# Attention scores on 32-row tiles of the array, Q masked by head parity, units of 256 queries, output clamps dropped

## The chip, the cores and the metric

The kernel runs on one core of one Trainium2 chip. The metric is the time of one execution on the device in microseconds (us), given as the median of several executions. Engine names are those of the profile: PE is the matmul engine, PEld its weight load, DVE VectorE, ACT ScalarE, POOL GpSimd. "Granted clock" is the PE clock in the clock records of the profile, with 1.00 for full speed. P·V is the matmul of the attention weights with V.

## The reference, cut to what matters

Two layers, each an attention block and a feed-forward block on the same weights. Inputs are bf16.

```python
def _A_ref(x, wqkv, wo):                  # B=1, S=2048, D=512
    H = 32; Dh = D // H; W = 256          # 32 heads of 16
    q, k, v = ...                         # from x @ wqkv
    scores = einsum("bhqd,bhkd->bhqk", q, k) * (Dh ** -0.5)
    mask = (0 <= idx_q - idx_k) & (idx_q - idx_k < W)   # causal, window of 256
    p = softmax(where(mask, scores, -1e9))
    return einsum("bhqk,bhkd->bhqd", p, v) @ wo         # heads side by side
def _B_ref(x, w1, w2):                    # Dff = 1792
    return relu(x @ w1) @ w2

x = x + _A_ref(layernorm(x), wqkv, wo);  x = x + _B_ref(layernorm(x), w1, w2)   # twice
```

A head has only 16 dimensions, so the contraction of a score matmul is 16 rows long on an array of 128 rows. All of the change turns on that.

## The kernel before

Heads lie 8 to a group `t` of 128 partitions. To score one head at a time with a matmul over all 128 rows, the kernel keeps copies of Q, `Qi`, that are zero in the rows of all other heads. Eight DMAs for each half of a chunk of 512 queries write the 16 live rows of each head into them. A unit of work is one block of 128 queries. Scores go to PSUM, the memory that PE writes its results to (a buffer of 512 fp32 columns there is called a bank below), ACT takes the exponential of eight heads at once, POOL clears what the mask forbids, and PE multiplies with V, which carries a column of ones for the row sums.

```python
    ptp = ...(name="ptp", bufs=5)
    ps_s = ...(name="ps_s", bufs=2, PSUM);   ps_acc = ...(bufs=1, PSUM)
    ps_w = ...(name="ps_w", bufs=1, PSUM)    # warm-up, output projection
    ps_d = ...(name="ps_d", bufs=2, PSUM)    # dense matmuls
    CLS = {"setup": 0, "s": 1, "a": 2, "q": 3, "f": 4}   # priorities: scores before attention before qkv before FFN
    # ... (cut)
    def isolate_q(QT, hfq):
        for j in range(8):
            nc.sync.dma_start(out=Qi[hfq][16 * j:16 * j + 16, :, j, :],
                              in_=QT[16 * j:16 * j + 16, :, hfq * 256:(hfq + 1) * 256])

    def attention_qblock(layer, qb, jq, chk):          # 128 queries
        # ... (cut) for a in range(2): for t in (2a, 2a+1): for kbi in range(3):
                        Sps = ps_s.tile([P, 2, 4, P], FP32, name="Sps")
                        for xh in range(2):
                            nc.tensor.matmul(Sps[:, xh]..., lhsT=KT[:, t, kcols],
                                             rhs=Qih[:, t, 4 * xh:4 * xh + 4, qcols], start=True, stop=True)
                        nc.scalar.activation(pt[:, kbi]..., Sps[:]..., ACT.Exp)
                # ... (cut) two affine_select on POOL, P·V matmuls, reciprocal, multiply into O
            ok1 = ...; ok2 = ...; ok = ...             # DVE: is the row sum within bounds
            nc.gpsimd.tensor_scalar(out=O[:], in0=O[:], scalar1=1.0e18, scalar2=-1.0e18, op0=ALU.min, op1=ALU.max)
            nc.gpsimd.tensor_tensor(out=O3, in0=O3, in1=ok[:]..., op=ALU.mult)

    def attn_post(qb, O):
        nc.sync.dma_start_transpose(out=OT[:], in_=O[:]...)
        ps = ps_w.tile([P, 512], FP32, name="ps_w")    # output projection, its own bank
        # ... (cut) 4 matmuls with wo, add to x
```

While chunk k is in attention, the q, k, v matmuls of chunk k+1 and the FFN of chunk k-1 fill the gaps of PE.

## Time and profile before

| | before |
|---|---|
| median of 2 runs | 642.85 us (641.36 to 644.34) |
| span of the profiled run | 643.3 us |
| mean granted clock | 0.970 |
| six attention stretches | 158.9, 51.5, 39.9, 51.5, 52.2, 52.2 us |
| five dense stretches between them | 31.7, 24.7, 28.5, 24.7, 25.7 us |
| from the last score to the end | 75.5 us |

The stretches are read from the timeline of PE. Where the score matmuls stop for tens of microseconds a dense stretch begins, and where they come back it ends.

These are lines of the page of the kernel before: busy time of each engine in us, then three of its rows of 40 equal slices, in tenths (9 is 90% or more).

```profile
PE 576.2 (90%) x5053; PEld 282.8 (44%) x5053; DVE 321.1 (50%) x701; ACT 368.2 (57%) x407; POOL 367.7 (57%) x391
...
ACT  5667686999850399705870399705894079920000
...
PEclk8968996999999999999999999999999999999998
```

ACT shows the two kinds of stretch: near 9 in attention, near 0 in dense work. After the first quarter the granted clock is full, but for 3.41 us at 578 us and the last 4 us.

The groups of instructions of the kernel before follow. The columns are line, engine, operation, tiles, shape and count, then busy us and mean ns of one, then the idle time ahead of them in us and what ended most of it.

```profile
L225 ACT ACTIVATE pt<-Sps 128x1024 bf16<-128x1024 f32 x360 | 344.8, 1025 | 95.3 <-PE Sps L223 82.8
L223 PE MATMUL Sps<-Qi,KT 128*128 128x512 bf16 x720 | 218.9, 386 | 4.1 <-ACT pt L225 2.8
```

The 386 ns is one matmul from start to end. In the records matmuls overlap, so the cost is the distance from start to start, and the timeline of PE in the kernel before shows it (columns: start, us, engine, line, operation, tiles, count):

```profile
302.64 0.59 PE L223 MATMUL Sps<-Qi,KT 128*128 128x512 bf16 x2
303.07 0.59 PE L346 MATMUL ps_d<-xn2T,w 128*128 128x512 bf16 x2
303.50 0.59 PE L223 MATMUL Sps<-Qi,KT 128*128 128x512 bf16 x2
```

Each pair of 512-column matmuls takes 0.43 us, that is 0.215 us each. A score group and a dense pair cost the same.

The windows of an attention stretch, a dense stretch and the tail of the kernel before follow. The columns are window and length, busy us (count) of PE, PEld, DVE, ACT and POOL, granted clock, share of DMA and GB/s.

```profile
217.00:268.50 51.50, 48.45 (x511) 25.05 (x510) 21.49 (x45) 44.64 (x47) 39.68 (x40) 1.00 0.16 33
268.50:293.20 24.70, 23.24 (x154) 10.60 (x151) 17.31 (x42) 2.29 (x6) 7.17 (x9) 1.00 0.08 19
567.80:643.30 75.50, 64.63 (x333) 28.71 (x329) 32.88 (x61) 1.64 (x4) 13.29 (x20) 0.95 0.21 33
```

An attention stretch has 48.45 us of PE and 44.64 us of ACT in 51.5 us, at full clock. Both are nearly full, so by an estimate from these numbers shortening the scores on PE can gain about 7 us of the 51.5 (51.5 − 44.64) and no more: then ACT is the limit.

### The profile page before, as it was taken

Reading aid. Unit: us, or ns where it says so; the run is one execution under the profiler, and the core shown is the slowest. Engines: PE = TensorE matmul, PEld = TensorE weight load, DVE = VectorE, ACT = ScalarE, POOL = GpSimd, SP = SyncE. Lnnn points to the kernel's source line nnn. Section 1 sums busy time; section 2 is a strip of 40 time slices with the busy share of each in tenths; the row PEclk is TensorE's granted clock in tenths of the full one; section 3 lists DMA queues with packets and bytes.
Section 4 is the critical chain, followed back from the end, with each engine's and each line's share of the span. In section 5 each row is a group of like instructions: output and inputs, shape, how many; then the busy total and the mean of one; then the engine's idle time right before and its main releaser. Section 6 shows DMA issues by size and latency. Waiting matters only on the chain.

```text
span 643.3 us, 12352 instructions
## 1 busy us (share of the span) xinstructions
PE 576.2 (90%) x5053; PEld 282.8 (44%) x5053; DVE 321.1 (50%) x701; ACT 368.2 (57%) x407; POOL 367.7 (57%) x391
## 2 busy tenths in 40 slices
PE   6957979999989999999899999999998899979994
PEld 2323434544544444534453444534454344534442
DVE  2794533544465634476455634475443544436361
ACT  5667686999850399705870399705894079920000
POOL 2168778888861287815872287814887147851200
PEclk8968996999999999999999999999999999999998
DMA  9601121111002110102101110202102210131302
GB/s 316 202 22 34 31 55 42 26 34 43 10 9 42 45 31 10 43 8 50 34 11 41 42 34 11 42 10 52 23 10 57 36 25 9 19 59 16 58 8 39
DMA packets 69217, 27.10 MB, mean 42 GB/s; under 512 B 52512, under 2 KB 68640, under 8 KB 69152
## 3 DMA queue, kind: packets, MB, share of 16 engines
q1 hardware_dynamic: 63984, 19.94, 13.6%
q0 software_dynamic: 2304, 2.10, 2.2%
q10 hardware_dynamic: 2864, 4.19, 1.8%
q8 instruction: 41, 0.67, 0.5%
q14 instruction: 24, 0.20, 0.1%
HBM read 7.86 MB, written 2.10 MB: 15 GB/s over the span
## 4 chain that ended last, share of the span: by engine, by line
PE 32%; POOL 19%; DMA 11%; issue 10%; ACT 8%; DVE 4%; SPq 0%; POOLq 0%; ACTq 0%
DMA OT<-O 9%; ACT pt L225 8%; PE ps_d L353 7%; POOL pt L228 7%; PE Sps L223 5%; PE ps_d L346 5%; POOL O L259 4%; POOL pt L232 4%; PE ps_w L333 3%; PE ps_d L176 3%; PE acc L240 3%; PE ps_d L184 3%; PE ps_d L191 3%; POOL O L257 2%; DMA xn2T<-xnB 1%
## 5 line engine op out<-in xcount | busy, mean ns | idle before, releaser
L225 ACT ACTIVATE pt<-Sps 128x1024 bf16<-128x1024 f32 x360 | 344.8, 1025 | 95.3 <-PE Sps L223 82.8
L223 PE MATMUL Sps<-Qi,KT 128*128 128x512 bf16 x720 | 218.9, 386 | 4.1 <-ACT pt L225 2.8
L228 POOL TENSOR_SCALAR_AFFINE_SELECT pt<-pt 128x1024 bf16<-128x1024 bf16 x128 | 140.3, 1099 | 67.4 <-ACT pt L225 67.1
L232 POOL TENSOR_SCALAR_AFFINE_SELECT pt<-pt 128x1024 bf16<-128x1024 bf16 x112 | 122.2, 1091 | 34.4 <-ACT pt L225 31.4
L240 PEld LDWEIGHTS <-pt 128*128 128x128 bf16 x2880 | 100.2, 96 | 87.6 <-POOL pt L228 38.4
L240 PE MATMUL acc<-Vaug,pt 128*128 128x17 bf16 x2880 | 108.9, 171 | 26.4 <-POOL pt L228 20.7
L346 PE MATMUL ps_d<-xn2T,w 128*128 128x512 bf16 x448 | 123.9, 378 | 0.9 <-DVE hT L348 0.9
L348 DVE TENSOR_SCALAR hT<-ps_d 128x512 bf16<-128x512 f32 x112 | 77.1, 689 | 61.4 <-PE ps_d L346 61.0
L353 PE MATMUL ps_d<-w,hT 128*128 128x512 bf16 x448 | 105.7, 381 | 0.0
L223 PEld LDWEIGHTS <-KT 128*128 128x128 bf16 x720 | 64.3, 97 | 68.5 <-issue 16.8
L334 DVE TENSOR_TENSOR x_sb<-ps_w,x_sb 128x512 f32<-128x512 f32 x32 | 22.1, 692 | 102.2 <-PE ps_w L333 80.8
L353 PEld LDWEIGHTS <-hT 128*128 128x128 bf16 x448 | 43.2, 98 | 50.4 <-issue 1.9
L346 PEld LDWEIGHTS <-w 128*128 128x128 bf16 x448 | 39.8, 97 | 43.2 <-issue 5.7
L333 PE MATMUL ps_w<-wo,OT 128*128 128x512 bf16 x128 | 38.3, 390 | 18.4 <-DMA OT<-O 18.3
L162 POOL TENSOR_SCALAR xnB<-x_sb,rstdB,nbB 128x512 bf16<-128x512 f32 x32 | 24.4, 766 | 42.4 <-DMA xn2T<-xnB 25.5
L247 DVE RECIPROCAL chk<-acc 128x16 f32<-128x16 f32 x64 | 16.4, 256 | 56.8 <-PE acc L240 56.7
L162 POOL TENSOR_SCALAR xnA<-x_sb,rstdA,nbA 128x512 bf16<-128x512 f32 x28 | 21.4, 769 | 40.2 <-DVE nbA L150 37.7
L178 DVE CAST QT<-ps_d 128x512 bf16<-128x512 f32 x32 | 22.0, 689 | 37.2 <-PE ps_d L176 37.2
L147 ACT ACTIVATE lnvB<-mv4B,ln_bias 128x4 f32<-128x4 f32 x8 | 2.4, 296 | 66.2 <-DVE mv4B L143 66.2
L357 POOL DMA_DIRECT2D out_dram<-x_sb x16 | 9.1, 570 | 52.8 <-DVE x_sb L355 37.2
L176 PE MATMUL ps_d<-xnT,wqkv 128*128 128x512 bf16 x128 | 36.4, 399 | 2.6 <-DVE QT L178 1.8
L355 DVE TENSOR_TENSOR x_sb<-ps_d,x_sb 128x512 f32<-128x512 f32 x32 | 22.0, 689 | 28.4 <-PE ps_d L353 25.8
(62 smaller groups left out, 391.5 us busy)
## 6 DMA issues: line engine op xcount, KB each, us to landing
Qi<-QT SPq DMA_DIRECT2D x128, 32.0 KB, 2.0
w<-in_B_w_dram ACTq DMA_DIRECT2D x2, 1792.0 KB, 13.9
xst<-in_A_x_dram SPq DMA_DIRECT2D x4, 512.0 KB, 14.4
out_dram<-x_sb POOLq DMA_DIRECT2D x16, 128.0 KB, 2.3
wqkv<-in_A_wqkv_dram SPq DMA_DIRECT2D x3, 512.0 KB, 13.1
wo<-in_A_wo_dram ACTq DMA_DIRECT2D x1, 512.0 KB, 5.5
OT<-O SPq DMA_TRANSPOSE x32, 2.3
xn2T<-xnB SPq DMA_TRANSPOSE x32, 2.4
```

The source lines that it names most:

```text
L162: nc.gpsimd.tensor_scalar(out=xn[:], in0=x_sb[:, b, :], scalar1=rstd[:, j:j + 1], scalar2=nb[:, j:j + 1], op0=ALU.mult, op1=ALU.add)
L176: nc.tensor.matmul(ps[:], lhsT=wqkv[:, kc, t * P:(t + 1) * P], rhs=xnT[:, kc, :], start=(kc == 0), stop=(kc == KC - 1))
L223: nc.tensor.matmul(Sps[:, xh].rearrange("p j q -> p (j q)"), lhsT=KT[:, t, kcols], rhs=Qih[:, t, 4 * xh:4 * xh + 4, qcols], start=True, st ...
L225: nc.scalar.activation(pt[:, kbi].rearrange("p j q -> p (j q)"), Sps[:].rearrange("p x j q -> p (x j q)"), ACT.Exp)
L228: nc.gpsimd.affine_select(out=pt[:, 2], in_=pt[:, 2], pattern=[[0, 8], [1, P]], compare_op=ALU.is_ge, fill=0.0, base=0, channel_multiplier=-1)
L232: nc.gpsimd.affine_select(out=pt[:, 0], in_=pt[:, 0], pattern=[[0, 8], [-1, P]], compare_op=ALU.is_gt, fill=0.0, base=0, channel_multiplier=1)
L240: mm = nc.tensor.matmul(acc[:, h % 16, :], lhsT=pt[:, kbi, j, :], rhs=Vaug[:, slot(layer, kb), h, :], start=(ii == 0), stop=(ii == len(kbi ...
L259: nc.gpsimd.tensor_tensor(out=O3, in0=O3, in1=ok[:].to_broadcast([P, 32, 16]), op=ALU.mult)
L333: nc.tensor.matmul(ps[:], lhsT=OT[:, kc, :], rhs=wo[:, kc, :], start=(kc == 0), stop=(kc == KC - 1))
L346: nc.tensor.matmul(ps[:, n0:n1], lhsT=w1[:, kc, f * P:(f + 1) * P], rhs=xnT[:, kc, n0:n1], start=(kc == 0), stop=(kc == KC - 1))
L348: nc.vector.tensor_relu(hT[:, f, n0:n1], ps[:, n0:n1])
L353: nc.tensor.matmul(ps[:], lhsT=hT[:, f, j * P:(j + 1) * P], rhs=w2[:, f, :], start=(f == 0), stop=(f == NF - 1))
```

## The change

The intent is to stop computing with rows that are zero. A score matmul is to use 32 rows of the array alone, and two of them on different rows are to run side by side. A row tile of 32 holds two heads, so Q is written twice, once with the odd heads zeroed and once with the even ones, both by DVE with a parity mask; the `Qi` copies, their clearing and their DMAs go. The unit grows to 256 queries of 8 heads. The checks and clamps of the output go; the flag at the end, which sends a bad input through a slow exact path, stays. `acc` gets a second PSUM buffer in the place of `ps_w`: the output projection now rotates through `ps_d`.

```diff
-    ptp = ... bufs=5        ps_acc = ... bufs=1       ps_w = ... bufs=1
+    ptp = ... bufs=3        ps_acc = ... bufs=2
 # ... (cut)
-        Qi = [const.tile([P, 4, 8, 256], BF16, name=f"Qi{i}") for i in range(2)]
+        nc.gpsimd.iota(pidx[:], pattern=[[0, 1]], base=0, channel_multiplier=1)
+        # ... (cut) par[:, 0], par[:, 1]: 1 or 0 by bit 16 of the partition number
 # ... (cut)
-            nc.vector.tensor_copy(QT[:, t, :], ps[:])
+            for e in range(2):
+                nc.vector.tensor_scalar(out=Qz[:, t, e, :], in0=ps[:], scalar1=par[:, e:e + 1], scalar2=None, op0=ALU.mult)
-    def isolate_q(QT, hfq): ...
-    def attention_qblock(layer, qb, jq, chk):
+    def attention_pair(layer, m, jm, Qz, chk):
+        for t in range(4):
+                for x in kinds:
+                    for rp in range(2):
+                        Sps = ps_s.tile([P, 2, 512], FP32, name="Sps")
+                        # ... (cut) parts: one of 256 queries, or two of 128
+                        for kb, col, qo, w in parts:
+                            for r in range(2):
+                                rows = slice(32 * (2 * rp + r), 32 * (2 * rp + r) + 32)
+                                nc.tensor.matmul(Sps[:, r, col:col + 2 * w], lhsT=KT[rows, t, kslice(kb)],
+                                                 rhs=Qz[rows, t, :, q0 + qo:q0 + qo + w], start=True, stop=True)
+                        nc.scalar.activation(pt[:, x, 2 * rp:2 * rp + 2, lo:512], Sps[:, :, lo:512], ACT.Exp)
+            # ... (cut) four affine_select, P·V into acc [P, 2, 8, 17]
-            ok1 = ...  ok2 = ...  ok = ...
-            nc.gpsimd.tensor_scalar(out=O[:], ... op0=ALU.min, op1=ALU.max)
-            nc.gpsimd.tensor_tensor(out=O3, in0=O3, in1=ok[:]..., op=ALU.mult)
 # ... (cut) attn_post
-        ps = ps_w.tile([P, 512], FP32, name="ps_w")
+        ps = ps_d.tile([P, 512], FP32, name="ps_d")
```

## The prediction

> **What bounds the kernel now.** The page shows PE busy 90% of 643.3 us, ACT and POOL 57%, but this averages two kinds of stretch. Gaps between score matmuls in the timeline give six attention stretches (158.9, 51.5, 39.9, 51.5, 52.2, 52.2 us) separated by five dense stretches (24.7 to 31.7 us, no scores, ACT idle), and a 75 us tail. Start to start, a 512-column matmul takes 0.215 us and a P·V matmul 0.026 us. A 48-exp stretch holds 46 us of PE stream (48 × 2 × 0.215 scores, 25.4 other), and 48 exps at 0.945 us each (8 in 7.55 us) are 45.4 us of ACT. Both are equally loaded; the stretch takes 52. The first (132 exps) has PE 121, ACT 125, and takes 159. PE streams sum to 539 us; about 104 is waiting.
>
> **What the change does.**
> - Scores: 720 matmuls of 512 columns become 480 of 512 and 480 of 256, the same columns, two side by side on different 32-row groups. [...] No trace here has row tiles. The compiled order has about 350 separate score groups among 128-row work, so nearly every group pays two switches. I estimate 0.40 us per group (0.3 to 0.5)[...]. That saves 10 us, not 75.
> - ACT is unchanged, so attention stretches cannot go below 45.4 us (125 in the first).
> - POOL loses two output operations (0.62 + 1.05 us, 32 times, 53 us), which delay the output transpose and the selects.
> - DVE writes Q twice (+0.69 us, 32 times) and drops three check operations (36 us in all).
> - The Qi clearing (7.1 us ACT) and 128 Qi DMAs go: first exp about 4 us earlier.
> - acc gets two buffers, but the output projection now shares ps_d. In the compiled order its 16 matmuls come only at the end of the previous chunk's FFN, 96 P·V matmuls after them. Dense stretches grow from 22.3 to 25.3 us of stream; the last FFN's layer norm and transposes (5.8 us for four) now stand exposed after the last projection. I add about 9 us of tail stall, and 11 us of tail stream moved from earlier stretches.
>
> **Sum (us).** First score 24; first attention 141; five dense 29, 28, 30, 28, 28; attention 48, 37, 48, 48, 48; tail 95: 632. So most of the PE saving goes into switches, the ACT floor and a longer tail.
>
> **Predicted: 632 us**, 604 to 664. Faster by over 2% 0.45, within 2% 0.37, slower 0.18.
>
> **What would show each step.**
> - Score groups: start of a group's first matmul to start of the next other matmul, 0.40 us; above 0.43 dearer than before, below 0.3 nearly free switches.
> - Exps back to back at 0.945 us through a 48-exp stretch of 47 to 49 us.
> - First attention stretch 135 to 148 us.
> - PE waits of 5 us or more ahead of the last two FFN chunks.
> - POOL busy near 315 us, DVE near 305.
>
> **What would make it wrong.** Switches far cheaper or dearer; row tiles not side by side; the lower granted clock (0.88 between 40 and 120 us) going or spreading; strided selects over 1.09 us; the deferred projection stalling scores through the output buffers.

The sum: 24 + 141 + 143 (five dense) + 229 (five attention) + 95 = 632 us. But the 0.40 us per group, and with it the 10 us saved in these terms, were the author's guess. Measured at full clock were 0.41 to 0.43 us, and 0.21 us for the two switches (both below).

## The result, and the profile after

The changed kernel gives a correct result and takes 784.91 us (median of 2; 781.40 and 788.43) against 642.85. The ratio is 1.221, with a 95% interval of 1.206 to 1.236. Here and below, a ratio is the mean time of one kernel's fast runs over the mean of the other's fast runs of the same rounds, so it is not quite the ratio of the medians that are quoted. The prediction was 632.

Lines of the page of the changed kernel:

```profile
PE 670.5 (86%) x5217; PEld 254.0 (33%) x5293; DVE 316.4 (41%) x640; ACT 373.0 (48%) x413; POOL 316.6 (41%) x328
...
ACT  2477595797308772177208772087721777100000
...
PEclk9975985795798557975797557975579655878988
```

POOL fell from 367.7 to 316.6 us and DVE from 321.1 to 316.4, close to the 315 and 305 predicted. But PE is busy 94 us *longer*, though by the forecast it had less to do, and the row of the granted clock has a new pattern: wherever ACT shows 7 or 8 (attention), the clock goes to 5 (half). In the records of the trace the clock is 1.0 or 0.5 and nothing between. The mean is 0.747, and 0.734 in the other run.

The groups of the changed kernel (columns as before):

```profile
L230 ACT ACTIVATE pt<-Sps 128x1024 bf16<-128x1024 f32 (+1 forms) x368 | 357.9, 1017 | 151.9 <-PE Sps L227 148.4
L227 PE MATMUL Sps<-Qz,KT 32*128 32x512 bf16 x960 | 190.0, 443 | 14.9 <-ACT pt L230 11.6
```

An exponential takes what it took, 1017 ns against 1025. But ACT now waits 148.4 us for scores, against 82.8.

The windows of an attention stretch, the dense stretch after it and the tail of the changed kernel:

```profile
234.20:298.30 64.10, 60.39 (x480) 18.59 (x486) 16.78 (x32) 47.61 (x49) 38.94 (x39) 0.59 0.08 17
298.30:328.60 30.30, 27.46 (x201) 12.85 (x202) 21.52 (x48) 1.62 (x3) 1.62 (x2) 0.97 0.09 19
664.90:779.70 114.80, 80.66 (x417) 35.49 (x422) 44.96 (x83) 2.21 (x5) 14.17 (x22) 0.86 0.17 31
```

In the attention stretch PE has 480 matmuls where it had 511, and needs 60.39 us instead of 48.45, at a granted clock of 0.59. ACT, which should have become the limit, is busy 47.61 of 64.10 us. The same work, told by stretch:

| stretch, us | before | predicted | after |
|---|---|---|---|
| to the first score | 26.4 | 24 | 32.8 |
| first attention | 158.9 | 141 | 170.4 |
| other five attention stretches | 247.3 | 229 | 305.0 |
| five dense stretches | 135.3 | 143 | 156.8 |
| tail | 75.5 | 95 | 114.8 |
| sum | 643.4 | 632 | 779.8 |

More than half of the miss against the prediction (76 of 148 us) is in the five later attention stretches, and 29 more in the first. The timeline of PE in one such stretch shows the same groups at both clocks. At full clock, in the changed kernel:

```profile
244.98 0.39 PE L227 MATMUL Sps<-Qz,KT 32*128 32x512 bf16 x2
245.30 0.46 PE L261 MATMUL acc<-Vaug,pt 128*128 128x17 bf16 x12
```

And 9 us later, at half clock:

```profile
253.47 0.61 PE L227 MATMUL Sps<-Qz,KT 32*128 32x512 bf16 x2 [0.37 <-issue]
254.01 1.03 PE L356 MATMUL ps_d<-xn2T,w 128*128 128x512 bf16 x2
254.98 0.61 PE L227 MATMUL Sps<-Qz,KT 32*128 32x512 bf16 x2
```

The two score matmuls of a group do run side by side: in the records they start 3 to 6 ns apart. At full clock the next matmul starts 0.32 us after the group, at half clock 0.54 us. A dense pair takes 0.96 us to the next group (254.01 to 254.98) where it took 0.43 in the kernel before.

Two smaller changes stand at the ends. The first matmul in the timeline of the kernel before is

```profile
1.43 7.74 PE L115 MATMUL warm<-ident 128*128 128x512 bf16 x28 [1.43 <-POOL ident masks.py:199]
```

and in the changed kernel the same warm-up, and further on the two last chunks of the FFN, begin with these waits (last column: idle time before and what ended it):

```profile
14.02 7.66 PE L120 MATMUL warm<-ident 128*128 128x512 bf16 x28 [14.02 <-POOL ident masks.py:199]
...
701.39 0.59 PE L356 MATMUL ps_d<-xn2T,w 128*128 128x512 bf16 x1 [10.74 <-DMA xn2T<-xnB]
...
743.75 0.59 PE L356 MATMUL ps_d<-xn2T,w 128*128 128x512 bf16 x1 [10.79 <-DMA xn2T<-xnB]
```

The identity matrix is made by POOL, which now first waits 10.24 us for the DMA of `wqkv`, because the new constants moved it behind that wait in POOL's order. The two waits of 10.7 and 10.8 us were predicted ("5 us or more"): the output projection now comes late. The windows of the projection's line alone in the changed kernel, for the attention stretch and the dense stretch above, have the columns PE, PEld, clock, DMA and GB/s:

```profile
234.20:298.30 64.10, 0.00 (x0) 0.00 (x0) 0.59 0.08 17
298.30:328.60 30.30, 3.88 (x15) 1.51 (x16) 0.97 0.09 19
```

In the kernel before, the same view has 12 projection matmuls in the attention stretch and 4 in the dense one. Now there are none in attention. They all fall into the dense stretch, and after the last chunk the whole FFN has to wait for them.

**Theories.** The trace suggests that the low granted clock made the difference, but not why it fell, nor how much else was lost. *Theory 1, activity*: the clock follows how much of the array works, so 32-row tiles pull it down, and what counts is the rows. *Theory 2, drains*: the pauses at each change between 32-row and 128-row matmuls (0.37 us without a matmul ahead of the group at 253.47 us above) make PE look idle, and the clock follows that; then 64-row tiles would suffer as much, and tiles without changes not at all. *Theory 3, schedule*: the new unit and the late projection make PE wait, and the clock follows from that; then full rows would not cure it. The two traces leave room for all three. What they show of the clock is its two values and its steps: the records are 0.5 or 1.0, and each lasts a multiple of 3.41 us (10.24 to 58.03 us in the changed kernel, 3.41 to 471.04 in the kernel before; where the trace cuts one off, it is not counted). On what it depends they do not say.

### The profile page after: what moved, and what is told of

Read it like the earlier page. It is cut to its first block, busy times and chain, and to the rows that moved or that the text cites. A ratio compares the mean times of both kernels' runs of the same rounds, so it can differ in the third digit from the quotient of the medians.

```text
span 779.7 us, 12389 instructions
## 1 busy us (share of the span) xinstructions
PE 670.5 (86%) x5217; PEld 254.0 (33%) x5293; DVE 316.4 (41%) x640; ACT 373.0 (48%) x413; POOL 316.6 (41%) x328
## 4 chain that ended last, share of the span: by engine, by line
PE 67%; DVE 9%; issue 8%; POOL 6%; ACT 4%; DMA 3%; SPq 1%; POOLq 0%; DVEq 0%; ACTq 0%
PE ps_d L356 19%; PE Sps L227 17%; PE acc L261 10%; PE ps_d L363 10%; DVE Qz L184 4%; PE ps_d L343 4%; ACT pt L230 4%; PE ps_d L197 3%; PE ps_d L190 2%; POOL xnB L167 2%; PE ps_d L181 2%; DMA xnT<-xnA 2%; DMA xn2T<-xnB 1%; POOL pt L240 1%; DVE x_sb L379 1%
## 5 line engine op out<-in xcount | busy, mean ns | idle before, releaser
L230 ACT ACTIVATE pt<-Sps 128x1024 bf16<-128x1024 f32 (+1 forms) x368 | 357.9, 1017 | 151.9 <-PE Sps L227 148.4
L227 PE MATMUL Sps<-Qz,KT 32*128 32x512 bf16 x960 | 190.0, 443 | 14.9 <-ACT pt L230 11.6
L356 PE MATMUL ps_d<-xn2T,w 128*128 128x512 bf16 x421 | 175.5, 539 | 26.1 <-DMA xn2T<-xnB 21.5
L261 PE MATMUL acc<-Vaug,pt 128*128 128x17 bf16 x2880 | 114.6, 175 | 13.9 <-POOL pt L245 8.3
L261 PEld LDWEIGHTS <-pt 128*128 128x128 bf16 x2880 | 94.0, 101 | 97.1 <-issue 71.9
L363 PE MATMUL ps_d<-w,hT 128*128 128x512 bf16 x440 | 100.7, 379 | 0.5
L227 PEld LDWEIGHTS <-KT 32*128 32x128 bf16 x960 | 41.8, 98 | 178.2 <-issue 172.4
L184 DVE TENSOR_SCALAR Qz<-ps_d,par 128x512 bf16<-128x512 f32 x64 | 44.3, 743 | 20.7 <-PE ps_d L181 20.3
L152 ACT ACTIVATE lnvA<-mv4A,ln_bias 128x4 f32<-128x4 f32 x8 | 2.4, 296 | 96.0 <-DVE mv4A L148 96.0
```

What stands on the lines that cost most here:

```text
L184: nc.vector.tensor_scalar(out=Qz[:, t, e, :], in0=ps[:], scalar1=par[:, e:e + 1], scalar2=None, op0=ALU.mult)
L227: nc.tensor.matmul(Sps[:, r, col:col + 2 * w], lhsT=KT[rows, t, kslice(kb)], rhs=Qz[rows, t, :, q0 + qo:q0 + qo + w], start=True, stop=True)
L230: nc.scalar.activation(pt[:, x, 2 * rp:2 * rp + 2, lo:512], Sps[:, :, lo:512], ACT.Exp)
L261: mm = nc.tensor.matmul(acc[:, qi, j, :], lhsT=lhsT, rhs=Vaug[:, slot(layer, kb), h, :], start=(ii == 0), stop=(ii == len(terms) - 1))
L356: nc.tensor.matmul(ps[:, n0:n1], lhsT=w1[:, kc, f * P:(f + 1) * P], rhs=xnT[:, kc, n0:n1], start=(kc == 0), stop=(kc == KC - 1))
L363: nc.tensor.matmul(ps[:], lhsT=hT[:, f, j * P:(j + 1) * P], rhs=w2[:, f, :], start=(f == 0), stop=(f == NF - 1))
```

## The experiments

Twelve kernels ran, on three chips: e1 to e4, e5 to e8 and e9 to e12. The kernel before ran beside each set and took 643.35, 643.58 and 644.59 us (medians), so differences between the sets can be read to about 1 us. Where a result is wrong it is said. Such a kernel sends other values through the array than the right one; no run tests by itself whether values change the time. But the kernel before streams copies of Q in which 7 of 8 rows are zero, and the granted clock of its later attention stretches is 1.00.

### Whole array, half array (e1, e2)

Both change one line of the changed kernel. The compiled order of instructions is the same in both as in the changed kernel. Scores are wrong.

```diff
-                                rows = slice(32 * (2 * rp + r), 32 * (2 * rp + r) + 32)
+                                rows = slice(0, 128)                      # e1
+                                rows = slice(64 * r, 64 * r + 64)         # e2
```

> The changed kernel with each score matmul on all 128 rows instead of 32: same instructions in the same order on every engine, same columns, no change of tiling mode; the sums mix four heads, so the result is wrong on purpose. Tiles theory (the 32-row score tiles cost the TensorE clock): granted clock at 0.93 or more, 48-exp stretches near 52 us instead of 64, total 640 to 680 us. Schedule rival (unit of 256 queries, late output projection or lighter PE load cost the clock): clock stays near 0.75 and the total near 780.

> The changed kernel with each pair of score matmuls on two 64-row tiles (rows 0-63 and 64-127) instead of two 32-row tiles: same order, same columns, the same number of changes of tiling mode, but all 128 rows in use during a pair; the sums mix two heads, wrong on purpose. Activity theory (a pair of 32-row tiles uses half of the rows and counts as too little activity): clock 0.93 or more, total 640 to 680 us. Drain theory (the pauses at each change of mode make PE look idle): clock near 0.75, total near 780.

Measured: e1 674.71 us, ratio to the kernel before 1.049 (1.044 to 1.054); e2 679.03 us, ratio 1.054 (1.049 to 1.060). The row of the granted clock of e1, then that of e2:

```profile
PEclk9997899799999999999999999999999999969798
```

```profile
PEclk9995599599799899999999999999999799969798
```

The attention dips are gone in both, but for the first stretch (long ones in e2, short ones in e1 as in the kernel before) and two of 6.8 us in later stretches of e2 (from 231.8 and 528.8 us). The same holds for the windows of one later stretch (columns as before), e1 first, then e2:

```profile
219.00:265.50 46.50, 44.17 (x481) 26.27 (x488) 16.53 (x32) 44.11 (x49) 37.62 (x38) 1.00 0.12 24
```

```profile
367.50:413.60 46.10, 42.48 (x481) 17.54 (x488) 16.55 (x32) 43.69 (x49) 37.46 (x38) 1.00 0.12 24
```

Whether the two score matmuls of a group follow each other on the whole array (e1) or run side by side on its two halves (e2), the stretch takes the same: 46.5 and 46.1 us, against 64.1 with 32 rows. Of the 142.1 us that the changed kernel lost, 110.2 (784.91 − 674.71) come back with full rows, and 105.9 already with 64 rows. Theory 2 falls here, because e2 has the same number of changes of mode as the changed kernel; in its trace the next matmul starts 0.322 us after a group, as with 32 rows at full clock. Theory 3 falls as the cause of the clock by itself, because the order of instructions is the same. What theory 3 may still explain is the 31.9 us that remain.

### Streams of matmuls alone (e3, e5)

These kernels compute nothing. PE runs streams of matmuls from one weight tile, with no other engine and no wait between them. Between the parts of e3 full matmuls brought the clock back (1.00 from the start of B); in e5, B2, D2 and E2 begin at half clock on purpose, straight after a single 32-row tile repeated.

```python
A:  280 x [one 32-row tile]                  B: 280 x [32-row pair]         C: 280 x [four 32-row tiles]
D:  80 x [2 full, 32-row pair]               E: 80 x [2 full, 64-row pair]  F: 80 x [2 full, four 32-row tiles]
G:  80 x [2 full, 14 of 17 columns]          H: 2000 of 17 columns
e5: B2, D2, E2 as B, D, E but begun at half clock;  [1 full, n of 17 columns] for n = 40, 60, 90;
    T3: [one 32-row tile, 32-row pair];  M: [1 full, 32-row pair, 8 of 17 columns];  N: as M with a 64-row pair
```

> PE alone, no other engine works and nothing waits; eight streams of 60 us or so with full 128-row matmuls of 512 columns between them; the result is wrong on purpose. A: one 32-row tile repeated; B: two side by side; C: four side by side; D: two full matmuls then a pair of 32-row tiles, repeated; E: the same with a pair of 64-row tiles; F: the same with four 32-row tiles; G: two full matmuls then 14 of 17 columns; H: 17 columns alone. Activity theory: A and B fall to a clock of 0.5 although they never change mode, D falls, C, E and F keep 1.0. Drain theory: A, B and C keep 1.0; D, E and F fall. Schedule rival: none of D, E, F falls, since no wait for another engine is left. At full clock a D round should take about 0.85 us (0.43 for the two full, 0.42 for the pair as in the changed kernel).

> PE alone again, result wrong on purpose. Rule under test, read from the traces so far: in each window of 3.41 us, count columns streamed at full speed, weighted by the share of the 128 rows in use; below about 0.37 of the window PE gets half the clock in the next one, at 0.37 or more the full clock. So a load of 32-row pairs that held the full clock in e3_streams (0.50) must stay at half when it starts at half (0.25). Stretch B2 (pairs, begun at half clock): stays 0.5 to its end. D2 (2 full matmuls, then a pair of 32-row tiles, begun at half clock; 0.35): stays 0.5 or is late to recover. E2 (the same with 64-row tiles; 0.42): recovers within 10 us. One full matmul with 40 narrow ones (0.40): full; with 60 (0.365): at the edge; with 90 (0.34): half. M (pair of 32, 1 full, 8 narrow; 0.45) and N (64-row pair): full. Rival, that the clock follows the time in which PE streams anything, whatever the rows: B2 and D2 recover at once, since PE streams without pause, and M and N do not differ from B2.

The windows of e3, parts A to E and H in order; F and G, left out, ran at 1.00 (columns: PE, PEld, POOL, granted clock, DMA, GB/s):

```profile
42.50:159.60 117.10, 116.65 (x281) 40.29 (x282) 0.00 (x0) 0.52 0.00 0
184.40:245.30 60.90, 60.74 (x562) 27.20 (x563) 0.00 (x0) 1.00 0.01 1
268.80:329.70 60.90, 60.74 (x1122) 29.07 (x1123) 0.00 (x0) 1.00 0.01 2
353.60:421.90 68.30, 67.35 (x314) 16.51 (x320) 0.00 (x0) 1.00 0.00 0
446.00:514.40 68.40, 67.45 (x314) 16.61 (x318) 0.00 (x0) 1.00 0.00 1
...
717.40:774.30 56.90, 54.65 (x2002) 53.96 (x2002) 0.00 (x0) 0.54 0.02 4
```

Neither the activity forecast nor that of the drains held in full. Part A has no pause and no change of mode, and PE is busy 116.65 of 117.10 us; yet its clock fell 3.3 us after its start and stayed down (0.52). So drains are not needed for a fall. But B, with two tiles side by side, held full clock, and so did D, whose mode changes twice in each round: my activity expectation had said that B and D fall. So drains at this rate are not enough for a fall either, and that refutes them; the rows count, but the bar is lower than I had put it. The forecast of the schedule rival, that none of D, E and F falls, did hold. It does not save that theory as the whole cause: A fell with nothing to wait for, and e1 cured the clock with the order unchanged. And H, 128 rows but only 17 columns to each weight load, fell as A did (0.54).

Two costs can be read from the starts of the matmuls in this trace. C starts a round of four 32-row tiles every 0.2159 us, where one full matmul takes 0.2155: four tiles give 3.99 times the rate of one. The rounds of D start 0.858 us apart, where three full slots are 0.647; so going into row tiles and back costs 0.21 us. E (64 rows) has 0.860 us, the same.

The windows of e5 for B2, D2, E2, then n = 60 and n = 90 (PE, PEld, POOL, clock, DMA, GB/s; the first three begin 2 to 5 us early, in the single tiles before):

```profile
77.00:137.00 60.00, 60.00 (x273) 20.66 (x272) 0.00 (x0) 0.50 0.00 1
187.00:248.00 61.00, 61.00 (x163) 9.66 (x161) 0.00 (x0) 0.50 0.00 1
293.00:330.00 37.00, 37.00 (x159) 8.67 (x157) 0.00 (x0) 0.90 0.00 0
441.00:502.00 61.00, 61.00 (x1992) 54.46 (x1989) 0.00 (x0) 0.77 0.02 4
527.00:587.00 60.00, 60.00 (x1986) 54.68 (x1982) 0.00 (x0) 0.57 0.02 4
```

The first two lines are the main finding. B2 and D2 are the rounds of B and D, which held full clock in e3. Begun at half clock they stay at half clock for 60 us of gapless work. E2, the 64-row rounds, came back about 5 us after their start (0.90 over its window). With one full matmul to 40 narrow ones (not shown) the clock stayed full (1.00); with 60 it fell late (0.77), with 90 early (0.57); T3 fell (0.53), M and N held (1.00 each). Every forecast of e5 came true (for T3 there was none), and the rival's did not.

This suggests one quantity. Take from the trace of each run every matmul's start, columns and rows; give it columns × rows / 128 at the full rate (0.2155 us for 512 columns of 128 rows), and sum that over each 3.41 us window of the clock's records. A matmul that lies across two windows counts in each by its share. This share of the window, called *activity* here, is computed from the starts in all 14 traces; it is no view of the profile. The rule, read from the first six of them alone (the two kernels, e1 to e4), is that the next window's clock is full if the activity is over 0.37, and half if not. It is right for 2,764 of the 2,787 windows whose own clock and the next one's are on record (99.2%). To say that the clock stays as it is would be right for 94%, and the best threshold for PE's busy time, without the weight by rows, for 83%. All 85 windows at full clock that were followed by a fall had an activity of at most 0.38, and all 74 that were followed by a recovery at least 0.36. (Some matmul records are missing, 5217 to 5293 weight loads in the changed kernel, so the threshold isn't sharper than that.) e5 to e12: on these eight traces alone the rule is right for 1,547 of 1,560 windows.

The streams agree with estimates made by hand. A single 32-row tile is 32/128 = 0.25: it falls. A pair is 0.50 at full clock and holds, but at half clock the same pair takes 0.427 us instead of 0.216: 0.25, and in B2 it did not come back. D is (2 + 0.5) × 0.2155 / 0.858 = 0.63 at full clock; at half clock its round takes 1.507 us, which makes 0.36: it stays down, by a little. E is 3 × 0.2155 / 0.860 = 0.75, and at half clock, with a round of 1.506 us, 0.43: it comes back. So in these streams the clock acts as a **latch**, a switch that stays where it is until something pushes it: the same pairs ran on at 1.00 in B and at 0.50 in B2. In these numbers, one bar of 0.37 tells falls (at most 0.38) and recoveries (at least 0.36) alike, but at half clock even full matmuls back to back make only 0.50 (0.2155 / 0.427).

### The same tiles in the kernel before (e4)

The scores of the kernel before, with nothing else of the change. Wrong on purpose.

```diff
-  lhsT=KT[:, t, kcols], rhs=Qih[:, t, 4 * xh:4 * xh + 4, qcols]
+  rows = slice(32 * xh, 32 * xh + 32)
+  lhsT=KT[rows, t, kcols], rhs=Qih[rows, t, 4 * xh:4 * xh + 4, qcols]
```

> The kernel before with only its score matmuls cut to 32-row tiles (two per group, side by side; heads outside the rows get score 0, wrong on purpose); unit, masks, Qi copies, output operations and order stay. Tiles theory, activity or drain: clock falls to between 0.7 and 0.85, total above 700 us. Schedule rival: clock stays 0.97 and the total stays within 2% of 643.

Measured: 721.92 us, ratio 1.119 (1.114 to 1.124). The row of the granted clock of e4:

```profile
PEclk8955975555559985599559995599855998569998
```

This was expected (a clock of 0.7 to 0.85, over 700 us). The dips stand in every attention stretch here too. So 78.6 us (721.92 − 643.35, the median of the kernel before of the same rounds) come with row tiles alone, in another unit, another schedule and with the clamps. This supports that the tiles pull the clock down in another kernel with such a share of scores too.

### The rest: projection, identity (e6, e7, e9)

These three start from e1 (full rows, wrong), to look at the schedule without the clock.

```diff
 # e6 = e1 and
-    ps_acc = ... bufs=2
+    ps_acc = ... bufs=1;   ps_w = ... bufs=1
-        ps = ps_d.tile([P, 512], FP32, name="ps_d")          # attn_post
+        ps = ps_w.tile([P, 512], FP32, name="ps_w")
 # e7 = e1 and
+        make_identity(nc, ident[:])      # moved ahead of the scaling of wqkv; the parity constants go last
 # e9 = e6 and e7
```

> As e1_full_rows (wrong on purpose), but the output projection has a PSUM bank of its own again and acc one buffer instead of two. If the late output projection makes the long tail: tail after the last score 75 to 82 us instead of 111, the waits of 10.8 us ahead of the last FFN chunks gone, total about 640 to 650 (674.7 in e1). Rival, that the tail is long because attention ended early and left more FFN over: tail stays above 100 us and the total near 670. If acc's second buffer is what made the 46.5 us stretches short, they go back to 50 or more.

> As e1_full_rows, but the identity matrix is made before the Q weights are scaled and the parity columns are made last, so that POOL does not wait for the weights' DMA before it. Warm-up matmuls start at about 2 us instead of 14, first score at 26 to 28 us instead of 33, total 5 to 8 us under e1. Rival, that the start is bound by the loads anyway: first score stays at 32 to 33.

> e6 and e7 together: full rows (wrong on purpose), output projection in its own PSUM bank with one acc buffer, identity first. If the costs add: 634.1 minus 11 = 623 us (615 to 630), first score near 25, tail near 80, 48-exp stretches 45 us. What is then left of the change (unit of 256 queries x 8 heads, clamps dropped) can be set against e8 (615, clamps dropped alone): the unit itself is then worth nothing or less.

The window of the tail of e6, in the columns used before:

```profile
551.30:631.50 80.20, 70.76 (x362) 31.26 (x360) 36.76 (x63) 1.66 (x4) 13.43 (x21) 0.97 0.22 38
```

Measured: e6 634.10 us (ratio 0.985, 0.979 to 0.990), e7 663.69 (1.032, 1.027 to 1.037), e9 622.95 (0.967, 0.964 to 0.970). One run of the kernel before beside e6 and e7 took 2,358 us; it is not used. With its own bank the projection is back in the attention stretch (8 matmuls there, 8 in the dense one), the tail is 80.2 us instead of 110.8 in e1, and the whole gains 40.6 us. The second buffer of `acc` was not what made the stretches short: with one buffer they are 45.0 us, with two they were 46.5. But e6 changes the bank and the buffer together, and no run has one without the other; the 40.6 us belong to the two. Making the identity first starts the warm-up at 1.47 us, the first score at 24.4 instead of 33.0, and gains 11.0 us. The two add up: 634.10 − 622.95 is 11.15. Two of the totals were better than expected: e6 by 6 us, and e7 gained 11 instead of 5 to 8.

### The clamps alone (e8), and 64 rows on top (e11)

```diff
 # e8: the kernel before, without
-            ok1 = ...  ok2 = ...  ok = ...
-            nc.gpsimd.tensor_scalar(out=O[:], ...)
-            nc.gpsimd.tensor_tensor(out=O3, ...)
 # e11: e8, and scores on 64-row tiles
+                            rows = slice(64 * xh, 64 * xh + 64)
```

> The kernel before with only the output clamps and their check taken out (two POOL and three DVE operations per query block). If POOL sets the pace of the attention stretches: 48-exp stretches 47 to 50 us instead of 52, total 620 to 635. If it does not: stretches stay above 51 and total within 1% of 643.

> The best kernel so far (before without clamps, 615) with its two score matmuls of a group on two 64-row tiles side by side; correct, since rows outside a head are zero. All 128 rows stay in use during a group, half the score columns are saved, two changes of mode are paid. If a change of mode costs what the changed kernel shows at full clock (entry and exit together about 0.2 us, group 0.42 against 0.43): within 2% of 615, clock 0.93 or more. If the saved columns counted in full (0.215 us in 350 groups): 75 us less PE stream and 590 us or below.

Both results are correct. Heads 0 to 3 of a group lie in rows 0 to 63 and heads 4 to 7 in rows 64 to 127, so halves lose nothing. Measured: e8 615.37 us, ratio 0.955 (0.952 to 0.959). It beats both kernels, and is 5 us below the range expected. e11 616.11 us, ratio 0.956 (0.953 to 0.959): no difference. A window of an attention stretch of e8, in the columns used before:

```profile
206.70:255.30 48.60, 47.92 (x513) 25.81 (x512) 20.48 (x40) 44.00 (x48) 34.38 (x34) 1.00 0.17 35
```

POOL has 34.38 us in it instead of 39.68, and the stretch takes 48.6 us instead of 51.5. The groups tell why: PE's idle time ahead of P·V that a select on POOL ended fell from 20.7 to 8.9 us, and that ahead of the projection that the output transpose ended from 18.3 to 7.1. In e11 a group saves one slot of 0.2155 us and pays 0.21 us for going in and out, as in e3; what is left is nothing.

### 32 rows in the repaired schedule (e10), and with work to keep the clock (e12)

```diff
 # e10: the changed kernel with the two repairs of e9, 32-row tiles kept (correct)
 # e12: the changed kernel with one acc buffer, and after each score group
+                        kp = nc.tensor.matmul(keep[:], lhsT=wo[:, 0, 0:128], rhs=wo[:, 1, :], start=True, stop=True)
```

> The changed kernel with the same two repairs and its 32-row score tiles kept (result correct). If the tiles cost the clock whatever the schedule: granted clock 0.7 to 0.8, 48-exp stretches 60 us or more, total 725 to 745 us (785 minus 40 and 11), over 100 us above e9. Rival, that the clock fell because the output projection came late and left PE short of full matmuls in the stretches: clock above 0.9, total under 680.

> The changed kernel with one useless full-row matmul of 512 columns after each group of 32-row score tiles (into a bank of its own that nobody reads; acc one buffer to make room; result correct). It adds 352 matmuls, 76 us of PE stream at full clock. If the clock is lost because too few rows are in use per window: clock above 0.9, and the kernel gets faster in spite of the added work, 690 to 750 us against 785. If the clock is lost to changes of mode, to waits or to the schedule: clock stays near 0.75 and the time goes up to 850 us or more.

Both are correct. e10 has fast runs of 654.05 and 661.56 us and two of 664.25 and 675.74 that carry the label slow because they are over 1.5% above the fastest. The ratio of the fast ones is 1.021 (1.014 to 1.028). Neither expectation held in full. The total, under 680 us in all four runs, is the one of the rival, by which the late projection had left PE short of full matmuls; but the clock (0.84 to 0.88) lies between the two forecasts. I took 725 to 745 from the size of the effect in the changed kernel. The row of the granted clock of e10:

```profile
PEclk8975785569558999999999999999956999999998
```

And the windows of two like stretches of e10:

```profile
370.00:414.30 44.30, 42.92 (x530) 18.48 (x530) 16.99 (x35) 43.79 (x49) 34.71 (x34) 1.00 0.09 20
443.80:497.70 53.90, 52.87 (x529) 19.21 (x528) 17.15 (x35) 45.86 (x49) 35.76 (x35) 0.74 0.08 16
```

This pair shows the latch inside one execution. The same work takes 44.3 us when the clock holds and 53.9 when it falls in the middle. In the first stretch the activity of the windows is 0.42 to 0.64. In the second, one window at 466 us had 0.29, and the clock stayed at half until 500. That the four runs differ by 22 us goes with their mean clocks (0.876, 0.861, 0.861, 0.839, from the shortest run to the longest). With the projection back in the attention stretch, 8 full matmuls more in each, the activity lies mostly above the bar. So the tiles cost about 35 us there (the fast runs' mean 657.8 less the 622.95 of e9), or 40 by the median of all four, not 110. Slow here marks the runs in which the clock fell more often, so the fast ones alone make the cost look small. The late projection and the row tiles made each other worse.

The window of an attention stretch of e12:

```profile
245.50:291.10 45.60, 45.05 (x450) 19.80 (x450) 10.54 (x22) 43.96 (x51) 37.30 (x38) 1.00 0.13 24
```

e12 takes 734.85 us, ratio 1.141 (1.138 to 1.145), as the activity theory had forecast (690 to 750, clock above 0.9). It does 368 useless full matmuls, about 79 us of stream (368 × 0.2155), and is 50 us *faster* than the changed kernel. Its mean clock is 0.944 instead of 0.747, and its attention stretches with 48 exponentials take 45.6 us instead of 64.1. Adding work to PE pays back more than it costs here, which the waits of PE alone can't explain. (Its one `acc` buffer in place of two was not run alone.) It supports the activity theory and is no remedy: e1, with full rows and nothing useless, takes 60 us less.

## Why the prediction was wrong

The prediction was 632 us with a range of 604 to 664; the kernel took 784.9. The chance given to slower by over 2% was 0.18.

**The step that failed** is in the sum: "first attention 141; ... attention 48, 37, 48, 48, 48". All terms were costed with durations at full granted clock. The lower clock stood only in the list of risks ("the lower granted clock ... going or spreading"). In its place the runs showed a granted clock that depends on the rows in use. With full rows and the same order of instructions (e1) these stretches take 156.0, and 46.5, 37.0, 46.5, 46.6, 46.3 us. With 32-row tiles they take 170.4, and 64.1, 47.8, 64.4, 64.4, 64.3. The difference, 14.4 and 82.1 us, is most of the 110.2 us between the two medians.

The clock is not the whole miss. With full rows e1 still takes 674.71 us, 42.7 over the forecast and above its range. There the terms that were too small are the tail (110.8 for 95), the first attention stretch (156.0 for 141) and the start (33.0 for 24); they are taken up below.

The trace of the kernel before could have warned, if not told. Its later attention stretches held full clock, but all their scores use 128 rows: a pair counts as two full slots of activity there, and as half a slot after the change. The estimated activity of a stretch at full clock is about 0.80 with full rows, 0.58 with 64 and 0.47 with 32 (worked out from the matmuls of a stretch over its length in e1). Its mean is above 0.37, but a stretch isn't even: single windows of 3.41 us drop below it. In the changed kernel the windows from 225 us on have activities of 0.53, 0.51, 0.69, 0.60, 0.39 and 0.27; then the clock falls, at 245.7 us, and windows of 0.19 to 0.37 follow until the dense work gives 0.43 and full clock returns at 300.3 us.

Point by point:

- *"0.40 us per group (0.3 to 0.5)"*: about right at full clock, as the cost of a group. By the measure that the prediction named, from the group's first matmul to the next other one, it is 0.32 us; with the wait on the way in, which that measure leaves out, 0.41 to 0.43. That is 0.10 us for going in and 0.10 for coming out. The rounds of e3 agree, with 0.21 us for in and out; at half clock it is about 0.23 (rounds of 1.507 us in e5, less three full matmuls of 0.427). Why a change costs this was not shown. So the saving was less still than 10 us, and e1 against e2 (674.71, 679.03) and e8 against e11 (615.37, 616.11) show that tiles of half the array gained nothing in these two kernels. At half clock a group takes about 0.68 us.
- *Row tiles side by side*: right. The two matmuls of a group start 3 to 6 ns apart, and four tiles side by side in the sustained stream C of e3 gave 3.99 times the rate of one full matmul after the other.
- *"Exps back to back ... 47 to 49 us"*: wrong in the changed kernel, where ACT waited 148.4 us for scores, for the reason above. In e1 and e10 at full clock the stretches take 46.5 and 44.3 us, so ACT was in fact the floor that it was said to be.
- *"First attention stretch 135 to 148"*: measured 170.4. Clock explains 14.4 (e1: 156.0); the own bank another 5 (e6: 150.9). About 10 us of the term are a wrong size that no run separated.
- *"First score 24"*: measured 32.8. The prediction saw the DMAs that go, and missed that new constants change the order on POOL, so that the identity waits for `wqkv`. e7 showed 11.0 us for it.
- *"five dense 29, 28, 30, 28, 28"*: 31.1, 30.3, 33.0, 31.2, 31.2. The mechanism was right, the term 2 to 3 us short each. The first microseconds still run at half clock (0.97 over the stretch above); e1 has 29.0 to 31.5.
- *"tail 95", "PE waits of 5 us or more"*: the mechanism was right, its size was not: 114.8 us, with waits of 10.74 and 10.79 us. With the projection in its own bank the tail is 80.2 (e6).
- *POOL 315, DVE 305*: 316.6 and 316.4. POOL is right; DVE is 11 us off.

**The account.** Times are medians.

| step | us | change |
|---|---|---|
| the changed kernel | 784.91 | |
| 64-row tiles (e2) | 679.03 | −105.9 |
| full rows (e1) | 674.71 | −4.3 |
| projection in its own bank, one acc buffer (e6) | 634.10 | −40.6 |
| identity first (e9) | 622.95 | −11.15 |
| kernel before less clamps (e8) | 615.37 | |
| kernel before | 642.85 | |

The parts depend on the order in which they are taken: in the repaired schedule the tiles cost only some 35 us (e10). Dropping the clamps is worth 27.5 us by itself (642.85 − 615.37), which is the part of the change that pays. The 7.6 us between e9 and e8 (run on two chips) are what remains of the larger unit, the double writing of Q and the other selects against the Q copies by DMA; no run separated these.

**What stays open.** The rule with 0.37 is an empirical one, read from the first traces and tested on the later ones; that the hardware counts just this was not shown. Whether a 32-row kernel could be arranged to stay above it in every window was tried once (e10) and failed in some windows. One large change was tried to raise activity (e12), and it cost more than it would have to keep full rows.

## What to carry to other kernels

Before cutting matmuls down to a part of the array, work out what share of the array the stretch will use in each window of about 3.4 us, columns times rows. In these traces a window below about 0.37 was followed by half the clock, and in the changed kernel that lasted until dense work returned; that it is so in other kernels was not tested. A busy PE alone did not bring the clock back: B2 and D2 stayed at 0.50 for 60 us without a gap. A pair of tiles that replaced two full matmuls saved one slot of 0.2155 us and paid 0.21 us for the change of mode; the gain of 3.99 times was measured only in a long run of one mode (stream C), and no kernel here has such runs. A PSUM pool that is shared with background work can give the shared work that work's place in the order: here 40 us went that way, while two dropped operations on POOL and three on DVE, for each block of 128 queries, gave 27.5.
